# Dealing the rows of w_out over the DMA engines in another way, in a fused decode step of attention and a gated MLP

## The chip, the core and the metric

The kernel runs on one core of a Trainium2 chip. The core has TensorE (PE, with its weight loads PEld), VectorE (DVE), ScalarE (ACT), GpSimd (POOL) and SyncE (SP), and 16 DMA engines that move data between the chip's memory (HBM) and the on-chip memory of 128 partitions. The metric is the device time of one execution in microseconds; less is better. The time before is 663.28 us, the median of three runs (663.27, 663.28 and 664.64).

## The reference

```python
def _A_ref(x, k_cache, v_cache, wq, wo):                 # B = 4, D = 640, H = 32, Dh = 128, Sk = 4096
    q = (x @ wq).reshape(B, 1, H, Dh).transpose(0, 2, 1, 3)
    p = softmax(einsum('bhqd,bhkd->bhqk', q, k_cache) * Dh ** -0.5)
    return einsum('bhqk,bhkd->bhqd', p, v_cache)...reshape(B, 1, H * Dh) @ wo

def _B_ref(x, w_in, w_sp, b_sp, w_out):                  # F = 1728, Fh = 864
    z = gelu(einsum('bsd,df->bsf', x, w_in))
    z1, z2 = z[..., :Fh], layernorm(z[..., Fh:])
    g = einsum('ts,bsf->btf', w_sp, z2) + b_sp[None, :, None]
    return einsum('bsf,fd->bsd', z1 * g, w_out)          # w_out: 864 rows of 640

xn = layernorm(x)
return x + _A_ref(xn, ...) + _B_ref(xn, ...)
```

All weights and caches are bfloat16. The K and V caches are 134 MB each; w_q and w_o are 5.2 MB each, w_in 2.2 MB, and w_out 1.1 MB.

## The kernel before, in words

**One long stream of loads.** Nearly all time goes into bringing 282 MB from HBM. All large loads are issued by SP's queue, in the order w_q (L111), w_in (L114), the main part of w_out (L118), the rest of w_out in four pieces (L128), and then the K and V units and w_o (L167 and L175). A unit is all of K or V of one batch and eight heads: 128 partitions of 64 KB. Units land in five slots of half a unit each (`kv`, `SL`); the table `place` says which unit takes which two slots, and SP waits before a load until the slot's former content has been read. A load over 128 partitions is split evenly over the 16 DMA engines, eight partitions each. It has landed when the slowest of them is through.

**Per K unit.** DVE transposes the unit in eight pieces of 128x2048 words (L389) into one of two `kT` buffers, and PE multiplies each with the queries (L400, weights `QZ`) into the scores `S`. After four units (a group of heads) follow the softmax (L407 to L456) and the spreading of p into `Zb` (`z_fill`).

**Per V unit.** PE multiplies the unit with `Zb` (L474), and DVE reduces the result (L483 to L488). After a group, `emit_sel`, `emit_oT` and `emit_proj` (L496 to L524) fold it into `proj` with w_o. The last w_o part is loaded in four pieces (channels 0 to 4, 4 to 6, 6, 7), so that the closing matmuls (L517) can begin before the last has landed.

**The start.** While w_q and w_in stream in, DVE, GpSimd and ACT compute the layer norm of x (L191 to L208; the square is GpSimd's, L197), PE computes q (L287) and the hidden values of the MLP (L309 and L312), ACT applies the gelu (L318 and L322), and the gate follows (L334 to L353). Then L367 multiplies the gate's result `uT` with w_out into `proj`. GpSimd also makes all masks and identities (L181 to L271), in the order of the program.

**Where w_out lies.** Hidden column f sits in a slice `fc` of up to 128 partitions. The main part is `FA` = 4 slices of 128 partitions, 512 rows of w_out, in `w_out`. The other 352 rows lie in `w_rest`, on partitions 0 to 19 or 31 and 32 to 43 of `FR` = 9 slices, and these share their memory with the two `kT` buffers, so L389 can't begin before L367 is done. `RB` lists the four pieces as (block of 32 partitions, first slice, i, slices): a piece covers 4 x i partitions, and its source is written with i as the outermost dimension.

```python
RB = ((0, 0, 8, 7), (0, 7, 5, 1), (1, 0, 3, 7), (1, 7, 3, 2))
```

Of the kernel before, what the change touches and what calls it, by code (L numbers as in the profile page):

```python
# [11 lines left out]
F32 = mybir.dt.float32  # L12
BF16 = mybir.dt.bfloat16
# [3 lines left out]
def kernel(  # L17
# [19 lines left out]
    nc = tc.nc  # L37
    P = 128
    B, Sq, D = A_x.shape
    _, H, Sk, Dh = A_k_cache.shape  # L40
# [4 lines left out]
    NE = HG // HP  # L45
    M = P // HG
    T = Sk // M
    C2 = 2
    TC = 32
# [4 lines left out]
    G = HG * B  # L54
    F2 = B_w_in.shape[1]
    Fh = F2 // 2
    FA = 4
    FR = 9
    RB = ((0, 0, 8, 7), (0, 7, 5, 1), (1, 0, 3, 7), (1, 7, 3, 2))
    NRP = 44  # L60
    assert Fh == FA * P + 4 * sum(i * c for _, _, i, c in RB)
    FC = FA + FR
    NOUT = A_wo.shape[1]
    NH = 2
    NO2 = NOUT // NH
# [3 lines left out]
    const = ctx.enter_context(tc.tile_pool(name="const", bufs=1))  # L69
    small = ctx.enter_context(tc.tile_pool(name="small", bufs=2))  # L70

    NKT = max(2 * TC * 32, 7 * NOUT // 2)
    ktpool = ctx.enter_context(tc.tile_pool(name="ktpool", bufs=2))
    ppool = ctx.enter_context(tc.tile_pool(name="ppool", bufs=2))
    ps_s = ctx.enter_context(tc.tile_pool(name="ps_s", bufs=1, space=bass.MemoryType.PSUM))
    ps_o = ctx.enter_context(tc.tile_pool(name="ps_o", bufs=2, space=bass.MemoryType.PSUM))
# [6 lines left out]
    def misc_ps(shape, dtype):  # L83
        misc_ctr[0] += 1
        return ps_m.tile(shape, dtype, tag="misc", name=f"misc{misc_ctr[0]}")


    SL = T * Dh // 2
    kv = const.tile([P, 5 * SL], BF16)

    def at_slot(i, n, off=0):
        return kv[:, i * SL + off:i * SL + off + n]
# [23 lines left out]
    nf = FA * P  # L116
    w_out = at_slot(2, FA * NOUT, n_in).rearrange("p (c n) -> p c n", c=FA)
    nc.sync.dma_start(out=w_out, in_=B_w_out[0:nf, :].rearrange("(p c) n -> p c n", p=P))  # L118
    w_rest = []
    for k, n in ((0, 7), (1, 2)):  # L120
        t = ktpool.tile([P, NKT], F32, tag="kT", name=f"w_rest{k}")[:NRP].bitcast(BF16)[:, 0:n * NOUT]
        w_rest.append(t.rearrange("p (c n) -> p c n", c=n))
    nc.gpsimd.memset(w_rest[1].rearrange("p c n -> p (c n)").bitcast(F32), 0.0)
    r_at = [nf]
    for q, c0, ni, n in RB:
        r_at.append(r_at[-1] + 4 * ni * n)
        k = c0 // 7
        nc.sync.dma_start(out=w_rest[k][32 * q:32 * q + 4 * ni, 0:n].rearrange("p c n -> p (c n)"),  # L128
                          in_=B_w_out[r_at[-2]:r_at[-1], :].rearrange("(r i c) n -> i r (c n)", r=4, c=n))

    NB = 32 * FC
    z_at = n_in + FA * NOUT

# [116 lines left out]
    for q in range(4):  # L250
        nc.gpsimd.tensor_copy(out=SelE[32 * q:32 * q + 32, :, q % 2, :],
                              in_=b8[32 * q:32 * q + 32, 8:8 + HP, None].to_broadcast((32, HP, P // HG)))
# [10 lines left out]
                          in_=ident_f[:].rearrange("p (q x c) -> p q x c", q=2, c=C2))  # L263
# [38 lines left out]

    w_z = w_in.rearrange("p c (a f) -> p c a f", a=2)
    z_ps = misc_ps([P, 2, FA, 32], F32)
    zr_ps = misc_ps([64, 2, 256], F32)
# [12 lines left out]
    nc.scalar.activation(out=zT[:, :, 0:FA, :], in_=z_ps[:], func=ACT.Gelu_apprx_tanh)  # L318
    for (q, c0, ni, n), f0, f1 in zip(RB, r_at[:-1], r_at[1:]):
        f0, f1 = f0 - r_at[2 * q], f1 - r_at[2 * q]  # L320
        for a in range(2):
            nc.scalar.activation(out=zT[32 * q:32 * q + 32, a, FA + c0:FA + c0 + n, 0:4 * ni].rearrange("p c (i r) -> p c i r", r=4),  # L322
                                 in_=zr_ps[32 * q:32 * q + 32, a, f0:f1].rearrange("p (r i c) -> p c i r", r=4, c=n),
                                 func=ACT.Gelu_apprx_tanh)

    one_bf = const.tile([1, P], BF16)
# [27 lines left out]
    uT = z_b[:, 1, :]  # L354
# [6 lines left out]
    for f0 in range(0, FC, 4):  # L361
        for hf in range(NH):
            for fc in range(f0, min(f0 + 4, FC)):
                n = P if fc < FA else NRP
                nb = 32 if fc == 1 and hf == 0 else RW
                u0, r0 = 32 * fc + 1 - hf, 32 * (fc % 2)
                nc.tensor.matmul(proj[r0:r0 + nb, 0:NO2], lhsT=uT[:n, u0:u0 + nb],  # L367
                                 rhs=(w_out[:, fc] if fc < FA else w_rest[(fc - FA) // 7][:, (fc - FA) % 7])[:, hf * NO2:(hf + 1) * NO2],
                                 start=(fc == 1 and hf == 0), stop=False)


# [9 lines left out]
    def emit_K(u, k):  # L381

        g, b = divmod(u, B)
        hh = first.get(u, 0) ^ (k // 4)
        qp, kh = k // 2 % 2, k % 2
        t0 = 2 * TC * (2 * hh + qp)
        kw = unit(("k", u), t0, t0 + 2 * TC).bitcast(F32).rearrange("p (t w) -> p t w", w=KW)[:, :, 32 * kh:32 * kh + 32]
        kT = ktpool.tile([P, NKT], F32, tag="kT", name="kT")[:, 0:2 * TC * 32]
        nc.vector.transpose(kT[:].rearrange("p (t r) -> p t r", r=32), kw)  # L389
# [4 lines left out]
        kb = kT[:].bitcast(BF16).rearrange("p (i t e m w) -> p i t e m w", i=2, e=NE, m=M, w=2)  # L394
# [132 lines left out]
    for i, item in enumerate(seq):  # L527
        if i + 1 < len(seq):
            key, u = seq[i + 1]
            load_unit(seq[i + 1])  # L530
            if key == "k" and u == 2 * B - 1:
                load_wo(u // B - 1)
        else:
            load_wo(NG - 3)
            load_wo(NG - 2)
            load_wo(NG - 1, (0, 4, 6, 7, 8))
        key, u = item
        g, b = divmod(u, B)
        if key == "k":
            done = b == B - 1 and g > 0  # L540
            for k in range(8):
                emit_K(u, k)
                if done and k == 1:
                    emit_sel(g - 1)
                if done and k == 2:
                    emit_oT(g - 1)
                if done and k == 5 and g == 1:
                    emit_proj(g - 1)
            if b == B - 1:
                if g < NG - 1:  # L550
                    fill_qz(g + 1)
                softmax(g)
        else:
            emit_V(u)
# [6 lines left out]
    for c, hf in ((0, 0), (1, 0), (0, 1), (1, 1), (2, 0), (2, 1)):  # L561
        p = min(c, 1)
# [49 lines left out]
```

## Time and profile before

| | |
|---|---|
| median of three runs | 663.28 us |
| span of the profiled execution (first to last instruction) | 661.2 us |
| median less that span | 2.1 us |
| moved by the DMA engines | 282.58 MB, mean 427 GB/s |
| busiest compute engine | DVE, 372.2 us (56%) |
| PE | 287.5 us (43%) |
| first packet of w_q | 1.73 us |
| k unit 0 landed | 45.06 us |
| last w_out matmul (L367) ends | 39.3 us |
| last w_o landing | 658.13 us |

The page gives no other time for the profiled execution than its span. The page's rows are read so: a group's row has its line, engine and operation, output and input by the program's names, how often, then the busy time, the mean of one in ns, and the idle time of the engine before it with what ended it. The DMA row has the mean busy share of the 16 DMA engines in each of 40 slices in tenths. In the view by windows, the columns are the stretch, its length, the busy time of PE, PEld, DVE, ACT and POOL with their counts, TensorE's granted clock, the busy share of the DMA engines, and GB/s. The queues are named by number: q1 is SP's, q10 is ACT's, and q8 and q14 fetch instructions.

### The profile page before, as it was taken

How to read it: one execution, taken by the hardware profiler on the slowest of the kernel's cores; microseconds unless marked ns; L12 is line 12 of the kernel's file. 1: busy time of each engine (PE TensorE's matmuls, PEld its weight loads, DVE VectorE, ACT ScalarE, POOL GpSimd, SP SyncE). 2: the span in 40 equal slices, each digit the busy share in tenths (PEclk: the TensorE clock that was granted, in tenths of full speed). 3: DMA queues.
4: the chain of work that ended last, by engine and by line, in shares of the span. 5: the costliest groups of instructions: out<-in, count | busy, mean ns of one | idle time of the engine just before them, and what ended most of it. 6: DMA issues, size and time to landing. Idle time of an engine off the chain costs nothing.

```text
span 661.2 us, 5415 instructions
## 1 busy us (share of the span) xinstructions
PE 287.5 (43%) x2247; PEld 106.6 (16%) x2247; DVE 372.2 (56%) x306; ACT 73.6 (11%) x145; POOL 67.0 (10%) x137
## 2 busy tenths in 40 slices
PE   0436656446062555235436065533706244551236
PEld 0211212112011121111112022110202112120113
DVE  2229999766191759718356286764629175971112
ACT  0300000341100000430200000070110000043200
POOL 3600000031200000130300000030110000003300
PEclk9857788669577587676758577875858769766678
DMA  9999999999999999999999999999999999999996
GB/s 372 452 446 420 420 447 438 429 444 417 436 436 433 428 425 437 433 436 445 416 432 433 432 421 450 427 432 429 437 440 433 424 433 416 445 444 429 419 420 285
DMA packets 6930, 282.58 MB, mean 427 GB/s; under 512 B 811, under 2 KB 1091, under 8 KB 1487
## 3 DMA queue, kind: packets, MB, share of 16 engines
q1 hardware_dynamic: 6879, 282.24, 99.0%
q8 instruction: 17, 0.28, 0.2%
q14 instruction: 6, 0.05, 0.0%
q10 hardware_dynamic: 28, 0.01, 0.0%
HBM read 282.24 MB, written 0.01 MB: 427 GB/s over the span
## 4 chain that ended last, share of the span: by engine, by line
DMA 77%; DVE 9%; issue 8%; PE 4%; ACT 0%; SPq 0%; DVEq 0%; ACTq 0%
DMA kv<-in_A_k_cache_dram 46%; DMA kv<-in_A_v_cache_dram 26%; DVE kT L389 8%; PE O L474 4%; DMA kv<-in_A_wo_dram 4%; DMA kv<-in_A_wq_dram 2%; DVE pT_t L456 0%; ACT Zb L437 0%; DVE m L407 0%; ACT p_bf L450 0%; PE S L400 0%; PE misc L411 0%; SPq L128 0%; PE proj L517 0%; DVE o_q L569 0%
## 5 line engine op out<-in xcount | busy, mean ns | idle before, releaser
L389 DVE STREAM_TRANSPOSE kT<-kv 128x2048 f32<-128x2048 f32 x128 | 282.8, 2275 | 128.1 <-DMA kv<-in_A_k_cache_dram 128.1
L400 PE MATMUL S<-kT,QZ 128*32 128x512 bf16 x1024 | 187.1, 498 | 261.9 <-DVE kT L389 261.9
L400 PEld LDWEIGHTS <-QZ 128*32 128x32 bf16 x1024 | 59.8, 110 | 387.5 <-issue 323.2
L474 PE MATMUL O<-kv,Zb 128*32 128x512 bf16 x1024 | 75.0, 458 | 56.4 <-DMA kv<-in_A_v_cache_dram 49.5
L437 ACT ACTIVATE Zb<-pT_t,MkE 32x128 bf16<-32x128 bf16 x120 | 60.8, 507 | 117.6 <-PE O L474 104.6
L483 DVE TENSOR_TENSOR om<-O,Mk 128x512 f32<-128x512 f32 x15 | 10.4, 692 | 93.8 <-PE O L474 93.8
L435 POOL TENSOR_SCALAR Zb<-pT_t,MkE 32x128 bf16<-32x128 bf16 x60 | 43.1, 718 | 138.6 <-PE O L474 126.1
L474 PEld LDWEIGHTS <-Zb 128*32 128x32 bf16 x1024 | 34.0, 113 | 97.3 <-issue 69.6
L450 ACT ACTIVATE p_bf<-S,negmax 128x1024 bf16<-128x1024 f32 x4 | 4.5, 1115 | 403.7 <-DVE negmax L417 403.7
L433 DVE TENSOR_SCALAR Zb<-pT_t,MkE 32x128 bf16<-32x128 bf16 x76 | 25.1, 330 | 2.3
L375 POOL COPY QZ<-qT 32x32 bf16<-32x32 bf16 x16 | 5.0, 315 | 188.9 <-PE S L400 188.4
L484 DVE TENSOR_REDUCE R<-om 128x128 f32<-128x512 f32 x15 | 15.3, 1021 | 0.5
L456 DVE STREAM_TRANSPOSE pT_t<-p_bf 128x1024 bf16<-128x1024 bf16 (+1 forms) x8 | 9.6, 1240 | 5.5 <-ACT p_bf L450 5.5
L461 POOL TENSOR_SCALAR rs<-MkB,rowsum 128x4 f32<-128x4 f32 x4 | 1.2, 299 | 112.7 <-ACT p_bf L450 112.7
L507 POOL MEMSET oT<- 128x66 bf16 x4 | 0.5, 146 | 96.6 <-PE proj L517 96.6
L407 DVE TENSOR_REDUCE m<-S 128x1 f32<-128x1024 f32 x4 | 4.9, 1224 | 6.0 <-PE S L400 6.0
L486 DVE TENSOR_SCALAR R<-O,Mk 128x128 f32<-128x128 f32 x1 | 0.3, 350 | 14.0 <-PE O L474 14.0
L496 PE MATMUL misc<-R,SelX 128*128 128x512 f32 x8 | 4.5, 644 | 7.2 <-DVE R L484 5.5
L287 PE MATMUL q<-kv,xnT 128*32 128x512 bf16 x40 | 4.3, 614 | 6.4 <-DVE xnT L208 6.4
L463 PE MATMUL misc<-rs,SelE 128*128 128x4 f32 x8 | 2.4, 365 | 10.4 <-POOL rs L461 10.4
L191 DVE CAST kv<-kv 8x640 f32<-8x640 bf16 x1 | 0.5, 482 | 10.7 <-DMA kv<-in_A_x_dram 10.7
L499 DVE TENSOR_TENSOR om<-misc,h 128x512 f32<-128x512 f32 x4 | 2.8, 692 | 4.9 <-PE misc L496 4.9
(102 smaller groups left out, 80.0 us busy)
## 6 DMA issues: line engine op xcount, KB each, us to landing
kv<-in_A_k_cache_dram SPq DMA_DIRECT2D x8, 4096.0 KB, 30.5
kv<-in_A_v_cache_dram SPq DMA_DIRECT2D x1, 6144.0 KB
kv<-in_A_wq_dram SPq DMA_DIRECT2D x1, 5120.0 KB
kv<-in_A_wo_dram SPq DMA_DIRECT2D x3, 1280.0 KB
kv<-in_B_w_in_dram SPq DMA_DIRECT2D x1, 2160.0 KB, 19.8
kv<-in_A_v_cache_dram SPq DMA_DIRECT2D x1, 2048.0 KB
kv<-in_B_w_out_dram SPq DMA_DIRECT2D x1, 640.0 KB, 20.9
kv<-in_A_wo_dram SPq DMA_DIRECT2D x1, 640.0 KB
```

The costliest lines, as they stand in the source:

```text
L375: nc.gpsimd.tensor_copy(out=QZ[r0:r0 + 32, :, :, :, 8 + 8 * hp], in_=qT[32 * g:32 * g + 32, NE * hp:NE * hp + NE].rearrange("p e a b -> p ...
L389: nc.vector.transpose(kT[:].rearrange("p (t r) -> p t r", r=32), kw)
L400: nc.tensor.matmul(S_ps[32 * q:32 * q + 32, i], lhsT=QZ[:, b, 2 * kh + w, e, w0:w0 + 32], rhs=kb[:, i, :, e, :, w], start=(b == 0 and k < ...
L407: nc.vector.tensor_reduce(out=m1[:], in_=S_ps[:].rearrange("p i t m -> p (i t m)"), axis=AX.X, op=ALU.max)
L433: nc.vector.tensor_scalar(out=dst, in0=src, scalar1=mk, scalar2=None, op0=ALU.mult)
L435: nc.gpsimd.tensor_scalar(out=dst, in0=src, scalar1=mk, scalar2=None, op0=ALU.mult)
L437: nc.scalar.activation(out=dst, in_=src, func=ACT.Copy, scale=mk)
L450: nc.scalar.activation(out=p_bf[:, M:M + NP], in_=S_ps[:].rearrange("p i t m -> p (i t m)"), func=ACT.Exp, bias=negmax[:, 0:1], scale=scal ...
L456: nc.vector.transpose(pT_t[:, j0:j1, :], blocks)
L474: nc.tensor.matmul(O_ps[32 * q:32 * q + 32, :, :], lhsT=Zb[b % 2][:, w].rearrange("p h c -> p (h c)"), rhs=vv[:, w * 4 * Dh:(w + 1) * 4 * ...
L483: nc.vector.tensor_tensor(out=om4[:], in0=O_ps[:], in1=Mk4[:, :, None].to_broadcast((P, 4, Dh)), op=ALU.mult)
L484: nc.vector.tensor_reduce(out=R, in_=om4[:].rearrange("p c d -> p d c"), axis=AX.X, op=ALU.add)
```

## The change

The main part of w_out shrinks to one slice (`FA` = 1, 128 rows, one row on each partition). The other 736 rows lie in twelve slices (`FR` = 12) of one tile `kT_t`, which takes the place of the two `kT` buffers (the transposes now use its two halves in turn). They come in seven pieces (`PC`: block of 32 partitions, first partition in it, k, rows of partitions per share, first slice, slices): two from SP's queue with k = 8 and k = 3, and five from GpSimd's queue with k = 4, 2, 3, 2 and 2. Between these, GpSimd issues three small loads of 512 bytes a partition into a tile `walk` that nobody reads, with k = 14, 2 and 3. GpSimd's eight DMAs are issued one after the other in a fixed order, right after its first memset. The words of `kT_t` under w_rest are set to zero first, by DVE (128 x 3840 words), where GpSimd had set 44 x 640; L367 then reads all 128 partitions of every slice. The second-stage products of the MLP come in four blocks of columns instead of two, and the gelu of the rest in fourteen activations instead of eight.

```diff
-    FA = 4
-    FR = 9
-    RB = ((0, 0, 8, 7), (0, 7, 5, 1), (1, 0, 3, 7), (1, 7, 3, 2))
-    NRP = 44
+    FA = 1
+    FR = 12
+    nf = FA * P
+    PC = ((0, 0, 8, 4, 0, 8), (1, 0, 3, 4, 0, 11), (1, 0, 4, 4, 11, 1), (1, 16, 2, 4, 0, 12), (2, 0, 3, 4, 0, 7),
+          (2, 24, 2, 4, 0, 12), (3, 24, 2, 4, 0, 7))
...
-    NKT = max(2 * TC * 32, 7 * NOUT // 2)
-    ktpool = ctx.enter_context(tc.tile_pool(name="ktpool", bufs=2))
+    NKT = 2 * TC * 32
...
+    kT_t = const.tile([P, 2, NKT], F32)
...
-    nc.gpsimd.memset(w_rest[1].rearrange("p c n -> p (c n)").bitcast(F32), 0.0)
...
-        nc.sync.dma_start(out=w_rest[k][32 * q:32 * q + 4 * ni, 0:n].rearrange("p c n -> p (c n)"),
-                          in_=B_w_out[r_at[-2]:r_at[-1], :].rearrange("(r i c) n -> i r (c n)", r=4, c=n))
+    w_words = kT_t[:].rearrange("p i n -> p (i n)")[:, 0:FR * NOUT // 2]
+    nc.vector.memset(w_words, 0.0)
+    w_rest = w_words.bitcast(BF16).rearrange("p (c n) -> p c n", c=FR)
+
+    def load_piece(eng, i):
+        q, x0, k, r, c0, n = PC[i]
+        p0 = 32 * q + x0
+        return eng.dma_start(out=w_rest[p0:p0 + k * r, c0:c0 + n].rearrange("p c n -> p (c n)"),
+                             in_=B_w_out[f_at[i]:f_at[i + 1], :].rearrange("(r i c) n -> i r (c n)", i=k, c=n))
+
+    NST = 256
+    walk = const.tile([28, 3 * NST], BF16)
+
+    def step(k, j):
+        return nc.gpsimd.dma_start(out=walk[0:2 * k, j * NST:(j + 1) * NST],
+                                   in_=B_w_out[0:2 * k, 0:NST].rearrange("(r i) n -> i r n", i=k))
+
+    for i in (0, 1):
+        load_piece(nc.sync, i)
+    sw = step(14, 0)
+    for go in (lambda: load_piece(nc.gpsimd, 5), lambda: load_piece(nc.gpsimd, 2), lambda: load_piece(nc.gpsimd, 3),
+               lambda: step(2, 1), lambda: load_piece(nc.gpsimd, 4), lambda: step(3, 2), lambda: load_piece(nc.gpsimd, 6)):
+        with tc.issue_after(sw.ins):
+            sw = go()
...
-        for q in range(2):
-            f0, f1 = r_at[2 * q], r_at[2 * q + 2]
+        for q, (f0, f1) in enumerate(fq):
             nc.tensor.matmul(zr_ps[32 * q:32 * q + 32, :, 0:f1 - f0], lhsT=xnT[:, c, :],
...
-                n = P if fc < FA else NRP
...
-                nc.tensor.matmul(proj[r0:r0 + nb, 0:NO2], lhsT=uT[:n, u0:u0 + nb],
+                nc.tensor.matmul(proj[r0:r0 + nb, 0:NO2], lhsT=uT[:, u0:u0 + nb],
...
-        kT = ktpool.tile([P, NKT], F32, tag="kT", name="kT")[:, 0:2 * TC * 32]
-        nc.vector.transpose(kT[:].rearrange("p (t r) -> p t r", r=32), kw)
+        kT = kT_t[:, k % 2]
+        nc.vector.transpose(kT.rearrange("p (t r) -> p t r", r=32), kw)
```

More of the change, by code (lines that the diff above doesn't have):

```diff
@@ L56 @@
     Fh = F2 // 2
-    FA = 4
-    FR = 9
-    RB = ((0, 0, 8, 7), (0, 7, 5, 1), (1, 0, 3, 7), (1, 7, 3, 2))
-    NRP = 44
-    assert Fh == FA * P + 4 * sum(i * c for _, _, i, c in RB)
+    FA = 1
[3 more added lines that the diff above has]
+          (2, 24, 2, 4, 0, 12), (3, 24, 2, 4, 0, 7))
+    f_at = [nf]
+    for _, _, k, r, _, n in PC:
+        f_at.append(f_at[-1] + k * r * n)
+    assert Fh == f_at[-1]
     FC = FA + FR
@@ L114 @@
     nc.sync.dma_start(out=w_in, in_=B_w_in.rearrange("(p c) f -> p c f", c=DC))
-    nf = FA * P
     w_out = at_slot(2, FA * NOUT, n_in).rearrange("p (c n) -> p c n", c=FA)
     nc.sync.dma_start(out=w_out, in_=B_w_out[0:nf, :].rearrange("(p c) n -> p c n", p=P))
[L119 to L122, printed above, removed]
-    nc.gpsimd.memset(w_rest[1].rearrange("p c n -> p (c n)").bitcast(F32), 0.0)
[L124 to L127, printed above, removed]
-        nc.sync.dma_start(out=w_rest[k][32 * q:32 * q + 4 * ni, 0:n].rearrange("p c n -> p (c n)"),
-                          in_=B_w_out[r_at[-2]:r_at[-1], :].rearrange("(r i c) n -> i r (c n)", r=4, c=n))
+    w_words = kT_t[:].rearrange("p i n -> p (i n)")[:, 0:FR * NOUT // 2]
[18 more added lines that the diff above has]
+            sw = go()
     NB = 32 * FC
@@ L304 @@
     z_ps = misc_ps([P, 2, FA, 32], F32)
-    zr_ps = misc_ps([64, 2, 256], F32)
+    zr_ps = misc_ps([P, 2, 256], F32)
+    fq = [(min(f_at[i] for i in range(len(PC)) if PC[i][0] == q), max(f_at[i + 1] for i in range(len(PC)) if PC[i][0] == q))
+          for q in range(4)]
     w_za = w_z[:, :, :, 0:nf].rearrange("p c a (q j i) -> p c q a i j", q=4, j=32)
@@ L318 @@
     nc.scalar.activation(out=zT[:, :, 0:FA, :], in_=z_ps[:], func=ACT.Gelu_apprx_tanh)
-    for (q, c0, ni, n), f0, f1 in zip(RB, r_at[:-1], r_at[1:]):
-        f0, f1 = f0 - r_at[2 * q], f1 - r_at[2 * q]
+    for (q, x0, k, r, c0, n), f0, f1 in zip(PC, f_at[:-1], f_at[1:]):
+        f0, f1 = f0 - fq[q][0], f1 - fq[q][0]
+        rows = slice(32 * q, 32 * q + 32)
         for a in range(2):
-            nc.scalar.activation(out=zT[32 * q:32 * q + 32, a, FA + c0:FA + c0 + n, 0:4 * ni].rearrange("p c (i r) -> p c i r", r=4),
-                                 in_=zr_ps[32 * q:32 * q + 32, a, f0:f1].rearrange("p (r i c) -> p c i r", r=4, c=n),
+            nc.scalar.activation(out=zT[rows, a, FA + c0:FA + c0 + n, x0:x0 + k * r].rearrange("p c (i r) -> p c i r", r=r),
+                                 in_=zr_ps[rows, a, f0:f1].rearrange("p (r i c) -> p c i r", r=r, c=n),
                                  func=ACT.Gelu_apprx_tanh)
@@ L363 @@
             for fc in range(f0, min(f0 + 4, FC)):
-                n = P if fc < FA else NRP
                 nb = 32 if fc == 1 and hf == 0 else RW
                 u0, r0 = 32 * fc + 1 - hf, 32 * (fc % 2)
-                nc.tensor.matmul(proj[r0:r0 + nb, 0:NO2], lhsT=uT[:n, u0:u0 + nb],
-                                 rhs=(w_out[:, fc] if fc < FA else w_rest[(fc - FA) // 7][:, (fc - FA) % 7])[:, hf * NO2:(hf + 1) * NO2],
+                nc.tensor.matmul(proj[r0:r0 + nb, 0:NO2], lhsT=uT[:, u0:u0 + nb],
+                                 rhs=(w_out[:, fc] if fc < FA else w_rest[:, fc - FA])[:, hf * NO2:(hf + 1) * NO2],
                                  start=(fc == 1 and hf == 0), stop=False)
@@ L393, in emit_K @@
         S_ps = state[("S", g)]
-        kb = kT[:].bitcast(BF16).rearrange("p (i t e m w) -> p i t e m w", i=2, e=NE, m=M, w=2)
+        kb = kT.bitcast(BF16).rearrange("p (i t e m w) -> p i t e m w", i=2, e=NE, m=M, w=2)
         w0 = 8 - (b * C2 + hh)
```

## The prediction

> **What bounds the kernel now.** I read the page first: span, busy shares, the DMA row of the 40 slices, the queues.
>
> ```profile
> span 661.2 us, 5415 instructions
> PE 287.5 (43%) x2247; PEld 106.6 (16%) x2247; DVE 372.2 (56%) x306; ACT 73.6 (11%) x145; POOL 67.0 (10%) x137
> ...
> DMA  9999999999999999999999999999999999999996
> ...
> q1 hardware_dynamic: 6879, 282.24, 99.0%
> q8 instruction: 17, 0.28, 0.2%
> q14 instruction: 6, 0.05, 0.0%
> ```
>
> No compute engine is above 56%, and the 16 DMA engines are busy in every slice but the last. The stream bounds the kernel; only its start, its gaps and its end can be improved. Then the end of the chain of waits.
>
> ```profile
> 633.07 23.45 DMA kv<-in_A_wo_dram
> 656.52 0.04 issue
> 656.56 0.44 PE proj L517 x4
> ```
>
> The end hangs on the landing of the last w_o pieces. A DMA has landed when its slowest engine has written its share, so I read the last microseconds by windows; the column before GB/s is the mean busy share of the 16 DMA engines.
>
> ```profile
> 653.00:654.00 1.00, 1.00 (x15) 0.58 (x16) 0.71 (x2) 0.00 (x0) 0.00 (x0) 1.00 0.89 360
> 654.00:655.00 1.00, 0.40 (x6) 0.15 (x3) 1.00 (x1) 0.00 (x0) 0.00 (x0) 1.00 0.87 355
> 655.00:656.00 1.00, 0.99 (x16) 0.70 (x16) 0.26 (x2) 0.00 (x0) 0.00 (x0) 1.00 0.77 303
> 656.00:657.00 1.00, 0.70 (x12) 0.40 (x10) 0.00 (x0) 0.00 (x0) 0.00 (x0) 1.00 0.53 200
> 657.00:658.00 1.00, 1.00 (x19) 0.61 (x14) 0.66 (x2) 0.00 (x0) 0.00 (x0) 1.00 0.19 69
> ```
>
> The engines do not finish together: some stop at 653.4, the last at 657.73. The unused share is 0.11 + 0.13 + 0.23 + 0.47 + (0.73 - 0.19) = 1.48 us per engine. This is the whole stake: bytes stay the same, so perfect levelling gains 1.4 to 1.5 us, 0.21% to 0.22%. A measurement of this kernel tells about 0.2% (1.33 us) from no change.
>
> **Who finishes late.** The trace has start, duration and size of every packet, without its engine. A packet starts 3 to 4 ns before the end of the one before it on its engine; followed from 21.3 us on, that gives 16 chains of 396 packets each without a hole. An 8,960-byte packet of seven w_out rows takes 335 ns start to start, 5,120 bytes 193, 1,280 bytes 52: 48 to 52 ns a row. The start tells the classes apart, since the four L128 DMAs land in eight, five, three and three shares, nested: three engines (I call them 0 to 2) carry all four, 100 rows of w_out in all; two (3, 4) carry 64, three (5 to 7) 60, eight (8 to 15) 32. Each 16 KB fetch of q8 then makes its engine 1.55 us later than the others, the 8 KB fetches of q14 make theirs 0.7 to 0.97 us later.
>
> Last packets end so: engines 0 to 2 at 656.63, 657.15, 657.30. Engine 3 or 4, hit by three q14 fetches, 657.64; two of 5 to 7, hit by q8 twice each, 657.59 and 657.62; the other two of 3 to 7 at 654.64 and 655.28. Of engines 8 to 15 two without a fetch at 653.44 and 654.11, five with two q8 fetches at 656.27 to 656.42, one with three at 657.73. (At 80 to 90 us three chains run within 30 ns of each other. I give the hits at 350 and 647.6 to the engine hit at 40.6, since q8's other hits come round every eighth fetch.) The q8 order is: three of 8 to 15, two of 5 to 7, three of 8 to 15. That is a round over engines 6 to 13, upward from 11 or downward from 10. I take upward: 11 has three hits.
>
> **The change, part by part.** The rows per engine become 88 (0 to 2), 44 (3), 88 (4, 5), 40 (6, 7), 36 (8 to 10), 8 (11 to 13), 84 (14, 15), if GpSimd's queue deals its shares to successive engines from 0 on, as the code's walk of 14, 2 and 3 shares counts it. In time, with 8 x 0.193 falling to 8 x 0.052 for the main part (-1.13 us on every engine), the rest at 48 ns a row and about 0.05 us for walk packets:
> engines 0 to 2: 3.28 becomes 3.83, so -0.53, latest end 656.77;
> engine 3: 1.55 becomes 1.79, -0.89, 656.75 if it is the one with q14;
> 4 and 5: 1.55 or 1.34 become 3.86, +1.2 and +1.4, at most 656.68;
> 6 and 7: 1.34 becomes 1.63, -0.84, 656.78;
> 8 to 10: 0 becomes 1.39, +0.26, 656.68;
> 11 to 13: -1.03, the late one 656.70;
> 14 and 15: 0 becomes 3.62, +2.49, at most 656.60.
> The last end moves from 657.73 to 656.78: 0.95 us. Everything behind it is fed by landings: matmuls of L517 wait for the landings at 654.97 and 656.52, the last ones for 658.13, and R and oT (ready at 655.29) follow the last v piece, whose slowest engines are the same. So 0.95 us reaches the end.
>
> **What is hidden, and its cover.** The start of the kernel:
>
> ```profile
> 2.90 0.10 POOL L187 MEMSET eps_t<- 128x1 f32 x1
> ...
> 12.88 1.24 POOL L197 TENSOR_TENSOR kv<-kv 8x640 f32<-8x640 f32 x1 [9.88 <-DVE kv L196]
> ...
> 36.49 2.83 PE L367 MATMUL proj<-w_rest,kv 44*8 44x320 bf16 x18
> ...
> 45.25 17.66 DVE L389 STREAM_TRANSPOSE kT<-kv 128x2048 f32<-128x2048 f32 x8 [10.00 <-DMA kv<-in_A_k_cache_dram]
> ```
>
> DVE gets a memset of 128x3840 words: from GpSimd's 128x1024 in 0.95 us about 3.6, from DVE's own 128x2048 transposes of 2.275 us about 4.3. It ends near 5 us; DVE waits until 10.71 anyway. Behind it wait the two SP pieces, and with them the first k load on SP's queue, which is needed only near 20.5 us (issued at 16.62 now, because a w_rest DMA ahead of it waited for w_q; that wait moves to the second k load, which waits for qT at 25 anyway).
> On GpSimd seven of its eight DMAs wait for the memset, and the identity and then L197 stand behind them. No row shows such a DMA; SP's L128 issues took 0.72 to 0.88 us each, the loads 0.33. Below: 8 x 0.33, all inside GpSimd's idle 9.88 us. Above: 8 x 2.3, which is where the cover ends. I take 1 us, near L128: done near 12.5, L197 late by 0 to 1 us.
> The added packets (76 rows on 14 and 15, 48 on 4 and 5) share the engines with w_q and w_in, so w_in lands up to 3.6 us later and the z matmuls behind it too. There are 10 more of them at 0.27 to 0.4 us partly overlapping, and 14 activations where 8 took 1.23: +0.92. The last w_out matmul moves from 39.3 to about 44 or 45; k0 lands at 45.06, so DVE may start 1 us late, not more. If the cover goes, the fourth transpose releases the third k load (54.27) later; the engines run dry near 58.7, so 4 us more are free.
> L367 reads 128 partitions where 44 stood, in the same 26 matmuls; I count that as nothing. The first transpose now also waits for GpSimd's pieces, landed by 25. The four extra instructions per z round shift the q8 fetches by some microseconds, not in number.
>
> [...]
>
> **The sum.** Span 661.23 - 0.95 = 660.28. The median of the three runs, 663.28, lies 2.05 above the profiled span; with the same around it: 662.33, -0.14%.
>
> **Rivals.** (1) The round runs downward: the engine with three hits is 10, and gets +0.26 instead of -1.03: last end 657.99, 663.5. For it: the hit order fits both ways. (2) The change does not do what it says: GpSimd's pieces go one partition per engine from engine 0 on. Then 0 to 2 get 123 rows (+1.0), 5 to 7 get 79 (+0.8): last end near 658.5, 664.1. (3) The other side: the round-robin does not start at 0, so the 76 rows meant for 14 and 15 fall on two engines that are full. These would end at 656.78 + 3.62 = 660.4: +2.7, 666.0. It decides as soon as the offset is not 0, as only 14 and 15 have that room. [...] (4) GpSimd's DMAs take over 2.3 us each, the mixer ends after 48.7, and the third k load comes too late: every microsecond beyond is lost, 665 with 3 us each. Against it: the idle 9.88 us and SP's short issues. (5) Levelling is better than my chains say, up to 1.43: 661.85.
>
> **How the numbers follow.** Forecast 0.57 (662.33, its own range 661.9 to 662.8), downward round 0.16, spread 0.09, offset 0.07, late start 0.05, perfect levelling 0.06. The range 661.8 to 664.2 holds the forecast, rivals 1, 2 and 5: 0.88, less what an unknown cost of GpSimd's queue around the span may add. Faster by over 0.2% needs less than 661.95: rival 5 and the lower edge of the forecast, 0.16. Slower by over 0.2% needs more than 664.61: rivals 3 and 4 and a tail of 2, 0.15. The rest, 0.69, is within.
>
> **What would show it.** Right: the busy share in the last 4 us falls from near 1 to 0 within 1.5 us, the last w_o landing near 657.2, DMA slices at 9 as before, L389 starting by 46. Wrong: two chains ending 2 us or more after the others (offset), the share tapering as now (spread, or fetches on other engines), a DMA slice below 9 near 60 us (late start).

## The result, and the profile after

The changed kernel takes 665.2 us (median of 19 runs, 664.72 to 667.11); the kernel before 663.3 (19 runs, 663.08 to 665.98). The ratio is 1.0027, 95% interval 1.0019 to 1.0035: slower by 0.27%, where 662.33 was predicted.

First the page of the changed kernel: span, DMA row of the 40 slices, and the queues.

```profile
span 663.0 us, 5456 instructions
...
DMA  9999999999999999999999999999999999999996
...
q1 hardware_dynamic: 6839, 281.80, 98.6%
q0 software_dynamic: 448, 0.47, 0.2%
q8 instruction: 17, 0.28, 0.2%
q14 instruction: 6, 0.05, 0.0%
```

The span grew by 1.8 us, the median time by 1.9. The stream has no hole: the row of nines is that of before. q0, GpSimd's queue, is new and moves 0.47 MB; q8 still has its 17 fetches. So the loss is not a hole in the middle. The last microseconds, in the view by windows (the column before GB/s is the busy share of the DMA engines):

```profile
655.00:656.00 1.00, 0.43 (x8) 0.17 (x3) 0.99 (x1) 0.00 (x0) 0.00 (x0) 1.00 0.86 344
656.00:657.00 1.00, 0.47 (x8) 0.34 (x9) 0.29 (x2) 0.00 (x0) 0.00 (x0) 1.00 0.77 291
657.00:658.00 1.00, 0.79 (x12) 0.41 (x9) 0.00 (x0) 0.00 (x0) 0.00 (x0) 1.00 0.17 67
658.00:659.00 1.00, 0.92 (x14) 0.65 (x15) 0.17 (x1) 0.00 (x0) 0.00 (x0) 1.00 0.13 49
659.00:660.00 1.00, 0.90 (x16) 0.40 (x12) 0.94 (x3) 0.00 (x0) 0.00 (x0) 1.00 0.01 5
```

A share of 0.13 is two of 16 engines. Most engines stop by 657.3, but two work on until 659.1. In the chain of waits the landing of w_o that the closing matmuls hang on comes at 658.04, where it was 656.52:

```profile
634.60 23.44 DMA kv<-in_A_wo_dram
658.04 0.04 issue
658.09 0.44 PE proj L536 x4
```

The packets, followed as chains as in the prediction, show the two. Numbers count q8's fetches in order of time; a "hit" is a fetch on that engine. The engine numbers in brackets are the code's count of the dealing; no packet carries one. Where two chains of one class cross, the ninth and seventeenth hit are given to the engine of the first.

| class in the changed kernel | chains | hits of q8 | last packet ends (us) |
|---|---|---|---|
| 88 or 84 rows (0, 1, 2, 4, 5, 14, 15) | 5 | none | 656.40 to 657.05 |
| the same | 1 | 2nd, 10th | 659.11 |
| the same | 1 | 3rd, 11th | 659.16 |
| 36 to 44 rows (3, 6 to 10) | 3 | two each (4th, 5th, 6th, and eight later) | 656.72 to 657.30 |
| the same | 2 | none | 653.75, 654.35 |
| the same | 1 | none; three of q14 | near 657.2 |
| 8 rows (11, 12, 13) | 2 | two each (7th, 8th) | 656.11, 656.97 |
| the same | 1 | three (1st, 9th, 17th) | near 657.3 |

The classes have the sizes that the code counts (7, 6 and 3 chains), so GpSimd's pieces went where they were meant to go. But two engines that were given most of the rows are hit twice each (3.1 us: in this profile a fetch took 1.02 to 1.11 us, and the packet behind it 0.46 to 0.55 us longer than others of its size), and two that were given few are not hit at all. The mean landing of the last load moved from 656.75 to 657.29 us, by 0.54: there is also something that makes all engines later.

### The profile page after: what moved, and what is told of

It is laid out like the page before. It is cut to its first block, busy times and chain, and to the rows that moved or that the text cites. A ratio compares the mean times of both kernels' runs of the same rounds, so it can differ in the third digit from the quotient of the medians.

```text
span 663.0 us, 5456 instructions
## 1 busy us (share of the span) xinstructions
PE 285.1 (43%) x2257; PEld 107.2 (16%) x2257; DVE 375.2 (57%) x307; ACT 74.5 (11%) x151; POOL 71.0 (11%) x144
## 4 chain that ended last, share of the span: by engine, by line
DMA 74%; DVE 13%; issue 11%; PE 2%; SPq 0%; ACT 0%; DVEq 0%; ACTq 0%
DMA kv<-in_A_k_cache_dram 65%; DVE kT_t L408 11%; DMA kv<-in_A_v_cache_dram 5%; DMA kv<-in_A_wo_dram 4%; PE O L493 1%; DVE kT_t L125 0%; DVE pT_t L475 0%; DVE Zb L452 0%; SPq L131 0%; DVE m L426 0%; ACT p_bf L469 0%; PE S L419 0%; PE proj L536 0%; DVE o_q L588 0%; DVEq L408 0%
## 5 line engine op out<-in xcount | busy, mean ns | idle before, releaser
L408 DVE STREAM_TRANSPOSE kT_t<-kv 128x2048 f32<-128x2048 f32 x128 | 282.8, 2276 | 126.5 <-DMA kv<-in_A_k_cache_dram 126.5
L419 PE MATMUL S<-kT_t,QZ 128*32 128x512 bf16 x1024 | 185.3, 494 | 261.4 <-DVE kT_t L408 261.4
```

Of the source, the lines that this page charges most:

```text
L408: nc.vector.transpose(kT.rearrange("p (t r) -> p t r", r=32), kw)
```

## The experiments

### Which part costs: GpSimd's queue alone, and an attempt to read the engines' numbers

The kernel before, with eight loads of GpSimd's queue as the change has them (32 shares of 1,024 bytes, into memory that nobody reads):

```diff
+    sw, p0 = step(14, 0), 28
+    for k in (2, 4, 2, 2, 3, 3, 2):
+        with tc.issue_after(sw.ins):
+            sw = step(k, p0)
+        p0 += 2 * k
```

> The kernel before with eight small loads from GpSimd's queue added (14, 2, 4, 2, 2, 3, 3, 2 shares of 1,024 bytes into a tile that nobody reads), w_out dealt as before. Theory (only the rows per engine count): the same as the kernel before within 0.1 us, 663.3. Rival (GpSimd's queue itself costs the time): about 1.8 us slower, 665.1.

Measured: median 663.84 against 663.41 for before, ratio 1.0001 [0.999, 1.0012]. The interval holds 1, but the profile has the last landings 0.46 us later in the mean (657.21 against 656.75), and already 0.45 at the first K unit. I first read this run as "the queue costs nothing"; the runs at the end of this section correct that.

To read the engine of each chain, sixteen small loads of one share each, every one of another size, from GpSimd's queue, in the changed kernel and in the one above:

```diff
+        for e in range(16):
+            n = 144 + 16 * e
+                return nc.gpsimd.dma_start(out=walk[3 * e:3 * e + 3, 0:2 * n],
+                                           in_=B_w_out[0:6, 0:n].rearrange("(r i) n -> i r n", i=2))
```

> The changed kernel with sixteen small loads from GpSimd's queue added in the middle of the stream, each of one share and of a size of its own (1,728 to 4,608 bytes), so that a chain of packets can be told by its engine's number. Theory (the fetches of PE's instructions fall on other engines than I took): the two chains that end last carry the 15,360-byte pieces and the marks of engines 14 and 15, and both are hit twice by q8; two of engines 8 to 10 have no fetch at all and end first. Rival (the pieces of GpSimd's queue sit elsewhere, the fetches where I took them): the two last chains carry marks of engines between 6 and 13. Rival (the queue itself costs time): no engine of 14 and 15 has a fetch, and they end with the others. Time as the changed kernel's, 664.8 to 665.3.

> The same kernel as the walk alone, with sixteen small loads of one share and of their own sizes in mid-stream, to number the chains of the old dealing. Theory: the q8 fetches hit the same numbered engines as in the changed kernel (14 and 15 among them, two of 8 to 10 free of them). Rival (the fetches move with the program): another set of engines. Time 663.3 to 663.5.

Measured: 674.67 and 675.59 us (one run each), where 664.8 to 665.3 and 663.3 to 663.5 were expected. In the first the loads were issued at 24 to 50 us, earlier than meant, and GpSimd stood behind their waits: its first step of the gate (L355) began at 50.63 us, where the changed kernel has it at 29.07, and with it the last w_out matmuls and the first transposes came late. The third slice of the DMA row falls to 6. Two of the stretches between 42 and 52 us in which the stream stands nearly still:

```profile
46.00:47.00 1.00, 0.00 (x0) 0.00 (x0) 0.00 (x0) 0.00 (x0) 1.00 (x2) 0.50 0.04 4
...
50.00:51.00 1.00, 0.00 (x0) 0.00 (x0) 0.00 (x0) 0.00 (x0) 0.95 (x4) 0.50 0.00 0
```

That cost 9.5 us against the changed kernel and 11.8 against the walk alone. The hole also cut the chains, so the marks named no engine: both runs failed as measurements of the map (which engines carry q8's fetches). The later runs read it in another way, by giving engines unequal shares.

### Moving the largest piece

The changed kernel, with the piece of 48 rows a share that it has on 14 and 15 put on 8 and 9, or on 9 and 10 (partitions 64 to 71 and 68 to 75); the walk is fitted to it:

```diff
-    PC = ((0, 0, 8, 4, 0, 8), (1, 0, 3, 4, 0, 11), (1, 0, 4, 4, 11, 1), (1, 16, 2, 4, 0, 12), (2, 0, 3, 4, 0, 7),
-          (2, 24, 2, 4, 0, 12), (3, 24, 2, 4, 0, 7))
+    PC = ((0, 0, 8, 4, 0, 8), (1, 0, 3, 4, 0, 11), (1, 0, 4, 4, 11, 1), (1, 16, 2, 4, 0, 12), (2, 0, 2, 4, 0, 12),
+          (3, 0, 3, 4, 0, 7), (3, 24, 2, 4, 0, 7))
```

On 9 and 10 the fifth piece reads (2, 4, 2, 4, 0, 12) instead.

> Changed kernel, but GpSimd's largest piece (48 rows a share, two shares) lies on engines 8 and 9 instead of 14 and 15: rows of w_out become 84 on 8 and 9, 36 on 10, 14 and 15, the others as they were. Theory (the instruction fetches fall on 6, 7, one of 8 to 10 and 11 to 15, so that 14 and 15 end last only because they have both fetches and 76 rows): 14 and 15 end 2.3 us earlier, near 656.8. If 10 is the one of 8 to 10 that has fetches, 8 and 9 end near 656.9 too, the last end is 656.7 to 657.0 and the time 662.3 to 662.6 (ratio to before 0.9985 to 0.999). If 8 or 9 has them, that one engine alone ends near 659.1 and the time is that of the changed kernel, 665.2 (1.0027). Rival (the time went into what GpSimd's pieces do elsewhere, or the pieces lie on other engines than counted): 665.2 here and in the sister run on 9 and 10.

> The sister run: the same piece on engines 9 and 10. Theory: near 662.4 if 8 is the engine of 8 to 10 with fetches, else one engine ends near 659.1 and the time is 665.2. At most one of the two runs can be fast; if neither is, 9 is the engine with fetches. Rival: 665.2 in both.

Measured: 665.16 us, ratio 1.0023 [1.0013, 1.0033], and 664.94 us, 1.0025 [1.0012, 1.0038]. Taken by the times alone, the rival would stand: 665.2 in both. The chains tell more. With the piece on 8 and 9 two chains are late again, now with the 3rd and 11th hit (659.03) and with the 5th and 13th (659.32); the 2nd falls on a chain with few rows. With the piece on 9 and 10 three are late: 3rd, 5th and 6th hit (659.19, 659.04, 659.18). So hit by hit:

| hit | changed kernel | piece on 8, 9 | piece on 9, 10 | engine |
|---|---|---|---|---|
| 1st, 7th, 8th | 8 rows | 8 | 8 | 11, 12, 13 |
| 2nd | 84 or 88 | 36 to 44 | 36 to 44 | 14 or 15 |
| 3rd | 84 or 88 | 84 or 88 | 84 or 88 | one of 0, 1, 2, 4, 5 |
| 4th | 36 to 44 | 36 to 44 | 36 to 44 | 3, 6 or 7 |
| 5th | 36 to 44 | 84 or 88 | 84 or 88 | 9 |
| 6th | 36 to 44 | 36 to 44 | 84 or 88 | 10 |

One map fits the three, and it is neither the prediction's (6 to 13) nor the one I had when these runs were made (which had 14 and 15 both hit). In these three profiles engine 8 and one of 14 and 15 have no hit. In my expectations here and below, "5" and "6" were the likely ones of their sets; later runs narrow them to 4 or 5, and to 3 or 6, and these dealings go no further, since the members of each pair carry nearly the same rows. The profile of before does: the two chains of its middle classes that q8 hits have 60 rows, not 64, so they are two of 5 to 7. If its round is the same (the durations below say so), they are 5 and 6, and the round goes upward as the prediction took it, but not over neighbours: 5, 6, 9, 10, then 11 to 13 and one of 14 and 15.

### More rows on 14 and 15

```diff
+    def more():
+        return nc.gpsimd.dma_start(out=walk[64:112, 0:NOUT],
+                                   in_=B_w_out[0:48, :].rearrange("(r i) n -> i r n", i=2))
...
+               lambda: step(14, 2, 32), more):
```

> Changed kernel, and 24 more rows of 1280 bytes from GpSimd's queue on engines 14 and 15, into memory that nobody reads (and two walk packets on 0 to 13). Theory (14 and 15 set the end, one for one): 24 times 48 to 52 ns, so 1.15 to 1.25 us more than the changed kernel, 666.3 to 666.5 (ratio to before 1.0045). Rival (the two late engines are not 14 and 15): these have over a microsecond of room, so 665.2 to 665.4 (1.0027).

Measured: 666.89 us, ratio 1.0053 [1.0038, 1.0068], 1.7 us above the changed kernel and above the 666.3 to 666.5 expected. The chain with the 2nd and 10th hit ends at 660.84, 1.73 us later; the other late one, which got no rows, at 659.77, 0.61 later. So 1.1 us are the 24 rows, as worked out, on an engine that is one of 14 and 15. The other 0.6 us came to both; this run also has two more loads in GpSimd's queue and SP's second K load issued at 31.96 us where it was 25.73, and which of these costs it was not tested.

### The dealing that the map asks for

The rows dealt so that no hit engine has more than 44: 88 rows on 0, 1, 2, 7 and 8, 8 rows on 13. First with one more piece from SP's queue (the new `PC`, against the changed kernel), then with that piece from GpSimd's (the lines below it, against the first):

```diff
+    PC = ((0, 0, 8, 4, 0, 8), (1, 0, 3, 4, 0, 11), (1, 0, 5, 4, 11, 1), (2, 0, 5, 4, 0, 8), (3, 0, 2, 4, 0, 12),
+          (3, 24, 2, 4, 0, 9))
...
-    for i in (0, 1, 2):
+    for i in (0, 1):
         load_piece(nc.sync, i)
```

> The 736 rows of the rest dealt by the engines that the runs so far point to as hit twice by q8 (5, one of 6 and 7, 9 to 12, one of 14 and 15) or three times (13): 88 rows on 0, 1, 2, 7 and 8, 44 on 3 and 4, 40 on 5, 6 and 9 to 12, 44 on 14 and 15, 8 on 13. Theory (5, 9, 10 and one of 14 and 15 are hit, and 6 rather than 7): no chain ends near 659 any more; by the ends measured so far 5 ends near 656.8, 9 to 12 near 657.2, the free heavy ones near 656.9, and 13 with three hits near 657.5, which is the last: 1.65 us before the changed kernel's 659.16, so 663.3 to 663.6 us (ratio to before 1.000 to 1.0005), and no gain on the kernel before. If 7 is hit and not 6, one chain alone ends near 659.7 and the time is 665.5 to 665.8. Rival (14 and 15 are both hit and the prediction's round over 6 to 13 is wrong in those alone, so that 7 is hit): 665.5 to 665.8 too.

> As the run before it, with the same rows on the same engines, but the third of SP's pieces (one row on 0 to 4) comes from GpSimd's queue, so that k0's load is issued at 6.6 us again and not at 20.9. Theory: the mean landing falls back by about 1 us to that of the changed kernel (657.3), the last packets end near 657.5 (13, with three hits) where the changed kernel had 659.16, the last landing near 658.0, the time 663.3 to 663.6 us (ratio to before 1.000 to 1.0005). The five chains with 88 rows have no q8 hit; the chain with 8 rows has the 1st, 9th and 17th. Rival (7 is hit): one chain ends near 659.7, 665.5 to 665.8.

Measured: 665.41 us, 1.0019 [1.001, 1.0028], and 665.29 us, 1.0024 [1.0014, 1.0034]. Both miss. In the first, SP's third piece waits for a w_q landing with the first K load behind it, which is issued at 20.88 us instead of 6.63, and the whole stream is 1 us late (mean last landing 658.27). In the second that is mended, but two chains leave the start late: one with 88 rows begins the first K unit at 27.11 us (the other four at 24.66 to 25.19), one of those with 40 to 44 rows, hit twice, at 24.09 (the other nine at 22.15 to 23.43). They end at 659.14 and 659.22. In both runs packets are slow in the start: the 15,360-byte packets of the piece on 7 and 8 take up to 0.70 us in the second and up to 0.98 in the first, against 0.573 in the changed kernel, and w_q's 40,960-byte packets beside them up to 2.32 and 2.41 us, against 1.55 at most there. That piece lay on partitions 96 to 103. One expectation below calls these foreign partitions, after an estimate of mine of which engine writes which; no run shows it. A third run has the same piece, with the rest as in the changed kernel:

```diff
-    PC = ((0, 0, 8, 4, 0, 8), (1, 0, 3, 4, 0, 11), (1, 0, 4, 4, 11, 1), (1, 16, 2, 4, 0, 12), (2, 0, 3, 4, 0, 7),
-          (2, 24, 2, 4, 0, 12), (3, 24, 2, 4, 0, 7))
+    PC = ((0, 0, 8, 4, 0, 8), (1, 0, 3, 4, 0, 11), (1, 0, 4, 4, 11, 1), (2, 0, 3, 4, 0, 7), (2, 24, 2, 4, 0, 12),
+          (3, 0, 2, 4, 0, 12), (3, 24, 2, 4, 0, 7))
```

> Changed kernel, with the 48 rows a share of the piece on 4 and 5 moved to 7 and 8, so that 5 has 40 rows, 4 has 40 or 44, 7 has 88 and 8 has 84; 14 and 15 keep their 84. Theory (5 and one of 14 and 15 are the changed kernel's two late engines): one chain alone ends near 659.1, with the 2nd and 10th hit, the next ones near 657.3; the time stays within 0.3 us of the changed kernel's 665.2. Rival (14 and 15 are the two): two chains end near 659.1 as before the move.

Measured: 665.02 us, 1.0027 [1.0017, 1.0037]; seven of the piece's packets take 0.67 to 1.07 us, and the first K unit lands at 47.48 where the changed kernel has 44.73. It says nothing on the question it was made for. Both dealings were run again with the piece on partitions 60 to 67, the one by the map as e12 (the diff is against the second dealing by the map; the walk and the gelu's pieces are fitted to it):

```diff
-    PC = ((0, 0, 8, 4, 0, 8), (1, 0, 3, 4, 0, 11), (1, 0, 5, 4, 11, 1), (2, 0, 5, 4, 0, 8), (3, 0, 2, 4, 0, 12),
-          (3, 24, 2, 4, 0, 9))
+    PC = ((0, 0, 8, 4, 0, 8), (1, 0, 3, 4, 0, 11), (1, 0, 5, 4, 11, 1), (1, 28, 2, 4, 0, 12), (3, 0, 5, 4, 0, 8),
+          (3, 24, 2, 4, 0, 9))
```

The other one moves its piece to (1, 28, 2, 4, 0, 12) in the same way.

> [...] In the runs before, 15,360-byte packets of that piece took up to 1.07 us where they take 0.573 elsewhere, and one engine came out of the start 2.4 us late. Theory (that lateness is the foreign partitions' doing): all packets of the piece take 0.57 us, the mean last landing is 657.3 to 657.4, the last packets end near 657.5 (13, hit three times), the time is 663.3 to 663.6 us (ratio to before 1.000 to 1.0005). Rival (7 is slow for another reason, or the map is wrong): one chain again near 659, 665.2.

> [...] Theory (5 and one of 14 and 15 are the changed kernel's two late engines): one chain alone ends near 659.1, with the 2nd and 10th hit, all others by 657.5; 665.0 to 665.3 us. Rival (14 and 15 are the two): two chains near 659.1.

Measured: 664.37 us (663.42 to 665.18), 1.0015 [1.0006, 1.0024], and 665.52 us, 1.0031 [1.0019, 1.0043]; the second is above the 665.0 to 665.3 expected. All packets of the piece now take 0.573 us, in both runs, no w_q packet is slow, and no chain leaves the start late. So the place of the piece was the second cost; why, no run shows.

The second of the two has one late chain alone, at 659.02, with the 3rd and 11th hit, and its count is one ahead: its first two hits both lie on engines with 8 rows. Shifted by that, it is one of 14 and 15 again. The other late engine of the changed kernel is gone with the 48 rows of 4 and 5: it was one of these.

The first, by windows:

```profile
655.00:656.00 1.00, 1.00 (x16) 0.56 (x11) 0.00 (x0) 0.00 (x0) 0.00 (x0) 1.00 0.88 348
656.00:657.00 1.00, 0.69 (x12) 0.52 (x10) 0.00 (x0) 0.00 (x0) 0.00 (x0) 1.00 0.80 296
657.00:658.00 1.00, 0.91 (x18) 0.52 (x15) 0.88 (x3) 0.00 (x0) 0.00 (x0) 1.00 0.08 27
658.00:659.00 1.00, 0.23 (x4) 0.02 (x3) 0.55 (x2) 0.00 (x0) 0.00 (x0) 1.00 0.00 0
```

This is the tail that the prediction described: the share falls from 0.80 to 0.08 from one microsecond to the next, the last packet ends at 657.45 and the last landing is at 657.89, 1.75 us before the changed kernel's. Of its chains none with 88 rows is hit, so 7 is free like 8, and the single chain with 8 rows (13) has the 1st, 9th and 17th hit, as expected. The profiled execution took 663.42 us, as forecast, but the other ten runs took 664.05 to 665.18: by the median the forecast of 663.3 to 663.6 missed.

### Why the runs scatter

17 hits on eight engines give one of them three. In the profiled execution of before, two of its 60-to-64-row engines have the 4th and 5th hit; in that of the changed kernel the engines in the same places of the round have the 3rd and 4th. So the round can be the same if in the execution of before it starts one engine earlier, as it does in the run with one late chain. The durations of the fetches show the same without any rows: after the first fetch, two successive ones of each eight take 1.015 to 1.026 us and all others 1.05 or more. This pair is the 3rd and 4th in the changed kernel and in the dealing by the map on partitions 60 to 67, the 4th and 5th in before, and in the three runs below the 8th and 9th, the 5th and 6th, and the 4th and 5th. So the start differs between profiled executions. Each kernel has only one of these; that it differs between executions of one kernel is inferred. If it does, the third hit falls on another engine each time, and a kernel's time changes with it. The test takes one fetch away: the score matmuls of two K units are left out (their scores are missing from the output; loads and transposes stay), which is 256 of PE's instructions.

```diff
         w0 = 8 - (b * C2 + hh)
+        if g == 0 and b in (1, 2):
+            return
         for w in range(2):
```

> The kernel before with the score matmuls of two K units left out (u = 1 and 2: 256 of PE's instructions, so one 16 KB fetch of q8 fewer; their transposes and loads stay, the scores lack these units). 17 fetches over eight engines give one engine three; 16 give each two. Theory (the round starts at another engine in each execution, so the third hit falls on 5 or 6, which end last with 60 rows, in two of eight executions: these are the runs near 664.6): no run above 664 any more, median 663.0 to 663.4. Rival (the scatter has another cause): a quarter of the runs near 664.6 as before.

> The changed kernel with the same 256 instructions left out. Theory: 5 and one of 14 and 15 are hit twice in every execution and end at 659.1: 664.8 to 665.3, and the runs above 666.3 (a third hit on one of these two, two of eight) are gone. Rival: they stay.

> [...] Theory: e12's profiled execution, with the third hit on 13, was its fastest at 663.42, and the other runs at 664.05 to 665.18 are those with the third hit on one of the seven engines with 40 to 44 rows. With 16 fetches every run ends like the fastest or a little earlier (last packets 657.1 to 657.4): 663.0 to 663.5, median 1.0 below e12's 664.37, none above 664. Rival: median still near 664.4.

The queue's row, the same in all three:

```profile
q8 instruction: 16, 0.26, 0.2%
```

| | 17 fetches | 16 fetches | ratio to before, with 16 |
|---|---|---|---|
| before | 22 runs at 663.01 to 663.61, five at 664.36 to 664.73 | all 11 at 663.04 to 663.44, median 663.21 | 0.9996 [0.9988, 1.0005] |
| changed | 664.72 to 667.11, median 665.2 | ten at 664.65 to 665.35, one at 666.01, median 664.73 | 1.0021 [1.0012, 1.003] |
| by the map, partitions 60 to 67 | 663.42 to 665.18, median 664.37 | 662.89 to 663.64, median 663.31 | 0.9994 [0.9985, 1.0003] |

The upper runs of before are gone, and the dealing by the map falls by 1.06 us to the time of its best run. The spans of the same runs say it more clearly, since the time outside the span varies as well:

| | spans with 17 fetches (us) | with 16 |
|---|---|---|
| before | 22 at 661.2 to 661.8, five at 662.6 to 662.9 | all at 661.3 to 661.6 |
| changed | 15 at 662.9 to 663.5, four at 664.3 to 665.1 | all at 662.7 to 663.3 |
| by the map, partitions 60 to 67 | two at 661.1 and 661.2, nine at 662.1 to 662.6 | all at 660.9 to 661.3 |

In before a third hit matters on the two hit engines with 60 rows (two places of eight; five of 27 runs were high). With the map's dealing seven of eight places carry 40 to 44 rows, and nine of eleven spans were high. The changed kernel's run at 666.01 has a span of 662.7: its excess lies outside the span.

Three things stay open:

- The time outside the span is 1.73 to 1.86 us in all runs of before that have a span on record, but 1.78 to 2.81 in the changed kernel (median 2.1) and 1.79 to 2.54 in the dealing by the map with 16 fetches (median 2.2); that dealing is 0.3 us shorter in its spans than before with 16 fetches (medians 661.1 and 661.4) and loses it again outside them. The cause is not known.
- Before has nine more runs, at 665.2 to 666.0, in the sets taken with the other experiments and in the first. A third hit there moves the end by some 1.4 us (657.6 plus 1.55, where the last end was 657.73), which is too little for them.
- The test takes PE work away with the fetch (287.5 us busy become 263.9). The lowest times of before stay the same (663.01 and 663.04), but the two were not tested apart.

### What GpSimd's queue costs

Twice the walk of the first run, and the same shares in two loads of sixteen:

```diff
+    for k in (14, 2, 4, 2, 2, 3, 3, 2):
+        with tc.issue_after(sw.ins):
+            sw = step(k, p0, NST)
```

```diff
-    sw, p0 = step(14, 0), 28
+    sw = step(16, 0)
+    with tc.issue_after(sw.ins):
+        step(16, 32)
```

> The kernel before and sixteen small loads from GpSimd's queue (twice the eight of the walk-only run, whose median was 0.43 us above that of before, its mean last landing 0.46 us). Theory (each load of this queue costs all engines time): twice that, 0.85 us, 664.1 to 664.4. Rival (a price paid once for using the queue): 663.7 to 663.9. Rival (the difference of the walk-only run was scatter, its interval held 1): 663.3 to 663.5.

> The kernel before and two loads of sixteen shares from GpSimd's queue, as many shares and bytes as the eight of the walk-only run. If the cost goes by the number of loads: a quarter, 0.1 us, 663.4 to 663.6. If it goes by shares or is paid once: 0.43 us, 663.7 to 663.9.

Their queue rows, first that of the run with sixteen loads, then that with two:

```profile
q0 software_dynamic: 512, 0.07, 0.1%
```

```profile
q0 software_dynamic: 64, 0.03, 0.0%
```

| loads, shares | median less that of before | mean last landing less that of before |
|---|---|---|
| 2, 32 | 0.25 us (1.0004 [0.9992, 1.0016]) | 0.42 us |
| 8, 32 | 0.43 us (1.0001 [0.999, 1.0012]) | 0.46 us |
| 16, 64 | 1.02 us (1.0018 [1.0007, 1.0029]) | 1.07 us |

In these runs the queue has a price: in the profiles of the eight-load and the sixteen-load run every one of the 16 last packet ends, taken in order, is later than in before (by 0.26 to 0.69 us and by 0.71 to 1.53), and twice the work costs about twice the time. Of the medians only that of sixteen loads is clear of noise. In the landings, one profile each, the price goes by shares rather than by loads; in the medians two loads lie between. It does not go by bytes alone: the changed kernel has the same eight loads and 32 shares with 0.47 MB and is 0.54 us later. The 256 packets of the eight-load run take only 0.22 us an engine by their own durations; where the rest goes is open.

## Why the prediction was wrong

**What held.** The stream bounds the kernel and its end is its slowest DMA engine: the last of a load's 16 landings follows the last packet's end (658.13 after 657.73 us in before, 659.64 after 659.16 in the changed kernel, 657.89 after 657.45 in the dealing by the map on partitions 60 to 67). GpSimd's shares fell where the code counts them: the dealing to successive engines from 0 on, a condition of the sum, gives classes of 7, 6 and 3 chains, and the profile has these. That excludes the offset (rival 3) and the spread of one partition per engine (rival 2), which would have put 123 rows on three engines, where no chain has more than 88. The hidden work stayed hidden; these rows of the timeline of the changed kernel have start, busy time, engine, line, operation and, in brackets, the idle time before:

```profile
1.59 3.26 DVE L125 MEMSET kT_t<- 128x3840 f32 x1 [1.59 <-PEq L615]
...
12.92 1.24 POOL L215 TENSOR_TENSOR kv<-kv 8x640 f32<-8x640 f32 x1 [3.34 <-DVE kv L214]
...
37.68 3.20 PE L386 MATMUL proj<-kT_t,kv 128*8 128x320 bf16 x21
...
45.05 2.31 DVE L408 STREAM_TRANSPOSE kT_t<-kv 128x2048 f32<-128x2048 f32 x1 [8.12 <-DMA kv<-in_A_k_cache_dram]
```

The memset took 3.26 us (3.6 to 4.3 expected), GpSimd's square began at 12.92 where it was 12.88 (late by 0 to 1 expected), the w_out matmuls ended near 41 (44 or 45 expected), and the first transpose began at 45.05, before 45.25. Rival 4, a late start, is out.

**The step that failed: "That is a round over engines 6 to 13, upward from 11 or downward from 10. I take upward."** The order of the hits by classes (three of 8 to 15, two of the middle ones, three of 8 to 15) was read right, and a round over eight neighbours was then laid over it, because it fitted. The rival that I priced for it, the downward round (rival 1), was inside the same assumption. The runs put in its place: 9 to 13, one of 14 and 15, one of 4 and 5 (5, with the profile of before), one of 3 and 6 (6, likewise); and free are 7, 8 and the others. The sum took 4 and 5 "at most 656.68" and 14 and 15 "at most 656.60" from chains without a fetch. Taken from chains with two it would have been right: 657.59 or 657.62, plus 1.4, is 659.0, measured 659.16; and 656.28 to 656.42, plus 2.49, is 658.8 to 658.9, measured 659.11. That is 2.4 us on the last end, most of the 2.87 us between 662.33 and 665.2; of the profiled execution's rest 0.3 lie between the last packet and the end of the span (3.5 us before, 3.8 now) and 0.2 outside the span. The prediction named the sign to look for ("two chains ending 2 us or more after the others") and put it down to another cause; "fetches on other engines" it named only as a reason for a tapering share, without a price.

**The term that was mis-sized: "about 0.05 us for walk packets".** GpSimd's queue made all engines about 0.45 us later when alone; the mean last landing rose by 0.54 with the change. In the two late engines about 0.2 of this is seen. It is also part of why the dealing by the map, whose tail is level, at its best only equals the kernel before: its last landing is 0.24 us earlier, where the prediction gave its own dealing 0.95. Another part is "with the same around it": the 2.05 us set a median beside a profiled span shorter than most, and the time around the span did not stay the same (1.73 to 1.86 us in before, a median of 2.1 in the changed kernel). The cause of that is open.

**What was not in the sum at all: the third hit.** "11 has three hits" was taken as fixed. It is one execution's; the durations of the fetches show that the start differs between the profiled executions, and the runs with 16 fetches fit a place that changes. So the forecast 656.70 for the late one of 11 to 13 could hold for some executions only. One small reading was off without effect: the first q14 fetch, at 34.4 us, made its engine 0.53 us later, not 0.7.

## What to carry to other kernels

In a kernel bound by its stream, a dealing of rows over DMA engines is only as good as the map of what else rides on them (here the wrong round was 2.4 us of the last end): read it by giving engines unequal shares in two or three dealings and intersecting the classes, and do not take a neat round that fits one profile for the map. Look at the chains as well as at the medians: three runs here had the time of the changed kernel for three different reasons. A scatter of runs by a fixed amount (here 1.0 to 1.5 us) may be one instruction fetch too many for an even round; one fetch less, with the 256 instructions behind it left out, was worth 1.06 us in one dealing here. Compare spans too: a part of what the changed dealings lost lay outside the span, where no chain shows it.

## What the runs showed that I had not expected

- q8's 17 fetches of 16 KB (16 with 256 of PE's instructions left out) fell on eight of the 16 chains in one order, in the changed kernel the 10th on the chain of the 2nd and the 11th on that of the 3rd, each making its chain about 1.55 us later; where the order starts differs between the profiled executions.
- With GpSimd's piece for 7 and 8 on partitions 96 to 103 its 15,360-byte packets took up to 1.07 us instead of 0.573, and the first K unit landed 2.7 us later. On partitions 60 to 67 all took 0.573.
- Small loads in GpSimd's queue made the last landings later out of proportion to their bytes: 0.03 MB in 32 shares by 0.42 to 0.46 us in the mean, 0.07 MB in 64 shares by 1.07, where 0.47 MB in 32 shares went with 0.54.
- The time outside the span is not a constant: 1.73 to 1.86 us in before, 1.95 to 2.04 with sixteen small loads of GpSimd's queue, up to 2.98 in the dealing by the map.
